# Attention and multiplicative feed-forward in float32: two-level gates from the fifth group on, and ScalarE's copies around the DMA turns

## The chip, the cores and the metric

The kernel runs on one core of a Trainium2 chip. The metric is the device time of one execution in microseconds (us), taken as the median over runs; lower is better. One execution was also recorded instruction by instruction, and all views below are of that one.

## The reference

Eight batches of linear attention with 8 heads of 64, 576 tokens each, an RMS norm per head, and then a feed-forward block on the 4608 tokens. All is float32.

```python
kv  = np.einsum('bhsd,bhse->bhde', k, v)
out = np.einsum('bhsd,bhde->bhse', q, kv)
rms = np.sqrt(np.mean(out * out, axis=-1, keepdims=True) + 1e-06)
x   = (out / rms * g_norm)             # then (B,H,S,D) -> (B*S, H*D) = 4608 x 512
a = x @ w1                             # 512 x 1024
b = x @ w2                             # 512 x 1024
h = a * b @ w3                         # 1024 x 1024
return h @ w_out                       # 1024 x 512
```

## The kernel before, in words

The product of w3 and w_out is folded into one matrix `w3o` at the start, so that each token needs the **gates** (x@w1 times x@w2, elementwise) and the **projection** (gates @ w3o). The tokens are worked on in nine groups of 512: groups 0 to 6 are the first 512 tokens of batches 0 to 6, then comes group 8 (the 64 tokens left over of every batch), and last group 7. Only the first group's order differs.

A group is one chain of TensorE (PE) work. The gates have 1024 columns, cut into four blocks p = 0..3 of 2 x 128. A block is done by `gates`, which calls `winograd`: a Strassen-Winograd scheme of one level, 7 products in place of 8, each of 4 matmuls 128x256. The sums that the scheme needs are made by VectorE: of the weights once (`sum_w`, kept in `ws0` to `ws3`), of x per group (`combine_x`, kept in `xc`), of the gates per block (`sum_ab`). ScalarE (ACT) takes three or four of the products out of PSUM (`keep`), and VectorE adds and multiplies the others (`done`, `multiply`). After the four blocks, `project_twice` makes the projection in two levels, 7 times 7 products of 2 matmuls 128x128; `sum_inner` makes its inner sums on VectorE, and the inner sums of w3o are loaded from HBM by `load_b` into three buffers (`streams`), 896 KB each.

In the last two groups (`TWICE`, 8 and 7) blocks 0 and 1 are made together in two levels by `gates_of_two`: two halves w (w1 and w2), each of 7 outer products of 7 matmuls 128x128. There the inner sums of the weights come from HBM (`prepare_w` writes them to `w_l2` in groups 3 and 4, `load_w` brings them back in three parts of 896 KB into the same three buffers), and the inner sums of x are made on GpSimd (POOL) by `sum_x` in 28 small operations. Order there: block 2, then blocks 0 and 1 in two levels, then block 3, then the projection.

While group T runs, the attention of batch T+1 is worked in between. `steps` makes eight lists of work, one for each call of `between`: `begin_kv` (k^T v), `finish` (q times kv and the norm, by `product` and `norm`), in odd batches `product_left` for the tokens left over of two batches. The norm is an ACT square into a tile `sq`, a VectorE reduction, an ACT square root, a VectorE reciprocal and a VectorE multiply that frees the PSUM bank. x and q are turned (transposed) by DMA: `turn_by_dma` copies a tile apart in 16-bit words, SyncE (SP) issues the DMA that turns it, and a second copy puts it together. All those copies but a few in the first group are POOL's.

[...] five of the pool `mm`, three of the pool `at`. A bank is handed out in turn, so a use waits for the readers of the use five (or three) back. PE, POOL and SP run in the order in which the code issues; VectorE and ACT are ordered by a scheduler, except where the code sets an order by hand.

Of the kernel before, what the change touches and what calls it, by code (L numbers as in the profile page):

```python
# [22 lines left out]
def kernel(  # L23
# [40 lines left out]
    KF = DF // P  # L64
    NH = KF // 2
# [254 lines left out]
    def attention(b):  # L320
# [41 lines left out]
        def q_by_dma(r):  # L362

            qT[r] = work.tile([P, 2, 2, P], FP32, name="qT")
            q_sb = loaded["q", b, r].rearrange("p e n -> p (e n)")
            to = qT[r].rearrange("p e i t -> p (e i t)")
            return turn_by_dma([q_sb], to, q_sb, [to], q_copy)
# [3 lines left out]
        def q_left_by_dma():  # L371
            st["qT"] = work.tile([P, NP, P], FP32, name="qT_left", bufs=1)
            src = q_left[b // 2].rearrange("p h d -> p (h d)")
            to = st["qT"].rearrange("p r t -> p (r t)")
            return turn_by_dma([src], to, src, [to], q_copy)

        def norm(o_ps, dsts):

            n, w = len(o_ps), o_ps[0].shape[1]
            inv = work.tile([P, n, w // D], FP32, name="inv")  # L380
            for i in range(n):
                sq = work.tile([P, G], FP32, name="sq")[:, 0:w]
                nc.scalar.activation(sq, o_ps[i], AF.Square)  # L383
                nc.vector.tensor_reduce(  # L384
                    out=inv[:, i], in_=sq.rearrange("p (h d) -> p h d", d=D), axis=AX.X, op=ALU.add
                )
            yield
            nc.scalar.activation(inv, inv, AF.Sqrt, scale=1.0 / D, bias=eps_col)
            yield
            nc.vector.reciprocal(inv, inv)  # L390
            for i in range(n):
                m, k = dsts[i].shape[1:3]
                nc.vector.tensor_tensor(  # L393
                    out=dsts[i],
                    in0=o_ps[i].rearrange("p (m k d) -> p m k d", k=k, d=D),
                    in1=inv[:, i].rearrange("p (m k) -> p m k", k=k).unsqueeze(3).to_broadcast(
                        [P, m, k, D]
                    ),
                    op=ALU.mult,
                )  # L400
# [24 lines left out]
        def product_left():  # L425
# [3 lines left out]
            o_ps = [bank(ps_at, "at"), bank(ps_mm, "mm")]  # L429
# [23 lines left out]
        def x_by_dma(h, copy=nc.gpsimd.tensor_copy):  # L453

            xn, x = st[h].rearrange("p i l m d -> p (i l) (m d)"), xT[b][:, h]
            flat = x.rearrange("p i r n -> p (i r n)")
            turned = st[h].rearrange("p i l m d -> p (i l m d)")
            half = [slice(r * G, (r + 1) * G) for r in range(2)]
            return together(
                turn_by_dma(  # L460
                    [xn[:, :, r * P:(r + 1) * P]], flat[:, half[r]], turned[:, half[r]], [x[:, :, r]],
                    copy,
                )
                for r in range(2)
            )

# [37 lines left out]
        def finish(h):  # L504
# [4 lines left out]
            q_two_by_dma, q_left_by_dma, x_by_dma, x_left_by_dma,  # L509
# [4 lines left out]
    def batch(b):  # L514
        if b not in batches:
            batches[b] = attention(b)
        return batches[b]

    def steps(b):
# [25 lines left out]
        odd = b % 2  # L545
        if b == 1:
# [12 lines left out]
        if b == 1:  # L559
# [19 lines left out]
            ends[5].append((end, "left", "u3"))  # L579
        else:  # L580
# [8 lines left out]
        if odd:  # L589
            fs[second].append((a.product_left,))  # L590
        if b == 1:
            turn(6, a.x_by_dma, 1)
            turn(7, a.x_left_by_dma, next_group=True)
        else:
            turn(5, a.x_by_dma, 1)
            if odd:
                turn(5, a.x_left_by_dma, next_group=more)
        if more:
            turn(7 if b == 1 else 5, batch(b + 1).q_two_by_dma, 0, 1, next_group=True)
            fs[7 if odd else 0].append((load_q_left, b + 1))  # L600
# [38 lines left out]
    def winograd(lhsT, rhs, chunks, done, between=lambda: None, keep_u3=True):  # L639
# [17 lines left out]
        def keep(name, ps):  # L657
            t = late_tile(name)[:, 0:4, :].rearrange("p (u a) n -> p u (a n)", u=2)
            copies.setdefault(name, []).append(nc.scalar.copy(t, ps))  # L659
            late[name] = t  # L660
# [109 lines left out]
    def gates(T, p, between, ready=lambda name: None):  # L770
# [4 lines left out]
        def multiply(name, one, two):  # L775

            dst = ab[int(name[1]) - 1][:, p, int(name[2]) - 1, :]
            if two is None:
                c = late_pool.tile([P, N], FP32, name="c21")
                nc.scalar.copy(c, one[:, 0, :])  # L780
# [15 lines left out]

    def prepare_w():

        for n, (name, _) in enumerate(PRODUCTS):
# [5 lines left out]
            for i, s in enumerate((s1, s2, s4)):  # L805
                at = (3 * n + i) * 2 * P
                nc.sync.dma_start(
                    out=w_l2[:, at:at + 2 * P].rearrange("p (w m) -> p w m", w=2), in_=s
                )
            yield  # L810

    def replace_a21():
        for name, _ in PRODUCTS:
            a11, _, a21, _ = w_blocks(name)
            nc.vector.tensor_sub(a21, a11, a21)

    loaded_w = []

    def load_w():
        n = len(loaded_w)  # L820
        t = streams[(n + 1) % len(streams)]
        nc.sync.dma_start(out=t, in_=w_l2[:, n * PART:(n + 1) * PART])
        loaded_w.append(t)
# [3 lines left out]
    def sum_x(T):  # L827
        if not x_sums:
            for name in ("k_sb", "v_sb", "q_sb"):
                for _ in range(2):  # L830
                    x_sums.append(inp.tile([P, 2, J * D], FP32, name=name))
            x_sums.append(work.tile([P, 2, 2, P], FP32, name="qT"))
            x_sums[:] = [
                t.rearrange("p a b -> p (a b)") if len(t.shape) == 3 else
                t.rearrange("p a b c -> p (a b c)") for t in x_sums
            ]
            x_sums[:] = [[t[:, i * P:(i + 1) * P] for i in range(4)] for t in x_sums]
        nc.gpsimd.tensor_copy(tick, late["p1"][:, 0, 0:1])
        for t, (_, name) in zip(x_sums, PRODUCTS):
            b11, b12, b21, b22 = (  # L840
                xb[T][name][:, c, i * P:(i + 1) * P] for c in range(2) for i in range(2)
            )
            t1, t2, t3, t4 = t
            nc.gpsimd.tensor_sub(t1, b12, b11)
            nc.gpsimd.tensor_sub(t2, b22, t1)
            nc.gpsimd.tensor_sub(t3, b22, b12)
            nc.gpsimd.tensor_sub(t4, b21, t2)

    places = []

    def gates_of_two(T):

        if not places:
            other = work.tile([P, 2, 2, NP // 2, N], FP32, name="xT")
            other = other.rearrange("p i j r n -> p (i j r n)")
            places.extend([other[:, 0:PART // 2], other[:, 1024:1024 + PART // 2]])
            places[:] = [t.rearrange("p (n t) -> p n t", t=P) for t in places]

        def products(n, w, ps, new):
            a_name, b_name = PRODUCTS[n]  # L860
            a11, a12, s3, a22 = (t[:, w] for t in w_blocks(a_name))
            s1, s2, s4 = (
                loaded_w[q // 7][:, q % 7 * 2 * P + w * P:q % 7 * 2 * P + (w + 1) * P]
                for q in range(3 * n, 3 * n + 3)
            )
# [3 lines left out]
            t1, t2, t3, t4 = x_sums[n]  # L869
# [10 lines left out]
            if w == 1 and n in (2, 4, 6):  # L880
                load_b()
            return ps

        def banks(pool, tag):
            return [bank(pool, tag).rearrange("p (i n) -> p i n", n=P) for _ in range(2)]

        def keep(t, ps):
            nc.scalar.copy(t[:, 0:4], ps[0])
            nc.scalar.copy(t[:, 4:7], ps[1][:, 0:3])
# [22 lines left out]
        for w in range(2):  # L912
            r1 = products(0, w, banks(ps_mm, "mm"), True)
            p1 = keep(late_tile("p1"), r1)
            r3 = products(1, w, banks(ps_at, "at"), True)
# [3 lines left out]
            z = keep(late_tile("u2"), r1)  # L919
            r2 = products(3, w, banks(ps_mm, "mm"), True)  # L920
            p5 = keep(places[1] if w else late_tile("p5"), r2)
# [7 lines left out]
            finish(keep(places[0], r1), w, 1, 0)  # L929
# [110 lines left out]
    def project_twice(T, last, ahead, load_after):  # L1040
# [43 lines left out]
        def keep(name, ps):  # L1084
            t = late_tile(name)
            nc.scalar.copy(t[:, 0:4], ps[0])  # L1086
            nc.scalar.copy(t[:, 4:7], ps[1][:, 0:3])
            return t

        def finish(z, half, j):  # L1090
# [8 lines left out]
            nc.vector.tensor_add(dst[:, 0], z[:, 3:6:2], z[:, 0:3:2])  # L1099
# [89 lines left out]
    w_l2 = dram.tile([P, 3 * PART], FP32, name="w_l2")  # L1189
    PRODUCTS = [  # L1190
        ("a11", "b11"), ("a12", "b21"), ("s2", "t2"), ("s1", "t1"), ("s3", "t3"), ("s4", "b22"),
        ("a22", "t4"),
    ]
    TWICE = (B, B - 1)

# [103 lines left out]
    for n, T in enumerate(groups):  # L1299
        pieces = steps(T + 1) if n + 2 < NG else iter([])  # L1300

        def between():
# [8 lines left out]
            if T == B - 2 and p == 2 and not replaced:  # L1311
                replaced.append(True)
                replace_a21()

        if T in TWICE:
            once = iter([T])
            gates(T, 2, lambda: [sum_x(t) for t in islice(once, 1)])
            run(sum_ab(2))
            in_order = tc.manual_schedule(engines={mybir.EngineType.DVE})
            in_order.__enter__()  # L1320
            gates_of_two(T)
# [3 lines left out]
        for p in range(NF):  # L1325
            if T in TWICE and p + 1 < NF:
                continue
            if T and p + 1 == NF:
# [10 lines left out]
                if T in TWICE:  # L1339
                    following["c12"] += of_two[:1]  # L1340
                    following["c22"] += of_two[1:]
                else:
# [38 lines left out]
            else:  # L1381
                ops = [step() for step in sum_ab(p)]
                with tc.issue_after(ops[-1].ins):
                    for _ in range({(3, 1): 2, (3, 2): 2, (4, 1): 2, (4, 2): 1}.get((T, p), 0)):
                        next(preparing_w)
        last = n + 1 == NG
        if T:
            project_twice(
                T, last, [] if last else combine_x(groups[n + 1]),
                load_w if not last and groups[n + 1] in TWICE else load_b,  # L1390
# [38 lines left out]
```

## Time and profile before

| what | value |
|---|---|
| median of 3 runs | 758.41 us (758.13 to 759.74) |
| the profiled execution | 758.72 us, its span 756.9 us |
| PE busy | 749.4 us of the span (99%) |
| VectorE busy | 589.4 us (78%) |
| ACT busy | 267.0 us (35%) |
| POOL busy | 164.1 us (22%) |
| HBM | 165 GB/s over the span |

Between the span and the execution's time lie 1.8 us that no instruction covers. "Busy" counts the time in which an engine executes; the mean granted clock of PE is 1.000. In lines of groups, `x` is the count of instructions; a float32 matmul of the program is recorded as two, so that one of 128x256 stands for 2 records.

### The profile page before, as it was taken

The numbers are of one execution on the slowest core, as the hardware profiler recorded it, in microseconds if no ns is written. First come the engines' busy times: TensorE is split into PE (matmuls) and PEld (weight loads), VectorE is DVE, ScalarE is ACT, GpSimd is POOL, SyncE is SP. The second block draws the span as 40 slices with busy tenths as digits, with TensorE's granted clock in tenths as the row PEclk, the third lists the DMA queues.
The fourth block names the chain that finished last, engine by engine and source line by source line (L and its number), as shares of the span: only waits on it lengthen the run. The fifth ranks groups of instructions, "written<-read, shape, count | busy, mean of one in ns | idle before, by whom it ended". The sixth has DMA issues, their size and how long they took to land.

```text
span 756.9 us, 14948 instructions
## 1 busy us (share of the span) xinstructions
PE 749.4 (99%) x5903; PEld 657.7 (87%) x5903; DVE 589.4 (78%) x1171; ACT 267.0 (35%) x492; POOL 164.1 (22%) x190
## 2 busy tenths in 40 slices
PE   8999999999999999999999999999999999999998
PEld 5455788888899889988998899889988999999997
DVE  7977999639888568758975897567776778996897
ACT  6777787312322232223222322232223223222321
POOL 0000000322511441144114410431143124006000
PEclk9999999999999999999999999999999999999999
DMA  9996954349997845675767567745743470465244
GB/s 319 344 334 177 273 163 102 85 104 271 336 299 248 225 114 177 223 205 141 218 218 210 155 192 223 208 103 173 224 125 53 150 225 28 146 211 186 87 152 139
DMA packets 146554, 143.20 MB, mean 189 GB/s; under 512 B 86580, under 2 KB 133812, under 8 KB 146484
## 3 DMA queue, kind: packets, MB, share of 16 engines
q1 hardware_dynamic: 144032, 127.82, 58.1%
q10 hardware_dynamic: 2452, 14.42, 5.7%
q8 instruction: 47, 0.77, 0.4%
q14 instruction: 23, 0.19, 0.1%
HBM read 105.78 MB, written 19.14 MB: 165 GB/s over the span
## 4 chain that ended last, share of the span: by engine, by line
PE 97%; DVE 1%; DMA 1%; ACT 1%; issue 0%; SPq 0%; ACTq 0%
PE mm L646 55%; PE mm L1075 23%; PE mm L625 7%; PE mm L875 5%; PE at L339 3%; PE at L415 2%; PE at L612 1%; PE at L875 1%; DMA raw<-in_moe_w_out_dram 1%; PE at L1126 0%; DVE ab L163 0%; PE at L358 0%; PE at L434 0%; DVE chunks L170 0%; SPq L198 0%
## 5 line engine op out<-in xcount | busy, mean ns | idle before, releaser
L646 PE MATMUL mm<-xT,w_sb 128*128 128x256 f32 x720 | 165.2, 380 | 0.0
L646 PEld LDWEIGHTS mm<-xT,w_sb 128*128 128x128 f32 x720 | 136.6, 191 | 18.3 <-issue 0.5
L646 PE MATMUL mm<-xc,ws 128*128 128x256 f32 x512 | 116.2, 380 | 0.0
L646 PEld LDWEIGHTS mm<-xc,ws 128*128 128x128 f32 x512 | 97.3, 190 | 13.7 <-ACT p L659 0.8
L296 POOL COPY xT<-xn 128x1024 uint16<-128x1024 uint16 x26 | 31.2, 1227 | 171.9 <-DVE xn L393 171.9
L784 DVE TENSOR_TENSOR c<-mm,u 128x512 f32<-128x512 f32 x32 | 22.0, 689 | 58.4 <-PE mm L646 58.4
L659 ACT COPY u<-mm 128x512 f32<-128x512 f32 x58 | 34.0, 585 | 93.4 <-PE mm L646 82.8
L659 ACT COPY p<-mm 128x512 f32<-128x512 f32 x66 | 38.7, 586 | 73.9 <-PE mm L646 68.5
L646 PE MATMUL mm<-xc,w_sb 128*128 128x256 f32 x256 | 61.4, 383 | 0.0
L625 PE MATMUL mm<-chunks,ab 128*128 128x512 f32 x128 | 60.1, 603 | 1.0 <-DVE chunks L173 1.0
L646 PE MATMUL mm<-xT,ws 128*128 128x256 f32 x240 | 57.4, 383 | 0.0
L785 DVE TENSOR_TENSOR ab<-c 128x256 f32<-128x256 f32 x96 | 53.8, 561 | 2.5
L646 PEld LDWEIGHTS mm<-xc,w_sb 128*128 128x128 f32 x256 | 48.0, 190 | 6.9 <-ACT u L659 0.3
L646 PEld LDWEIGHTS mm<-xT,ws 128*128 128x128 f32 x240 | 45.1, 190 | 6.2
L1075 PE MATMUL mm<-w3o_sb,ab 128*128 128x128 f32 x368 | 48.7, 276 | 0.0
L1075 PE MATMUL mm<-w3o_sb,raw 128*128 128x128 f32 x372 | 48.1, 276 | 0.0
L384 DVE TENSOR_REDUCE inv<-sq 128x8 f32<-128x512 f32 (+1 forms) x40 | 23.4, 627 | 30.0 <-ACT sq L383 30.0
L1075 PEld LDWEIGHTS mm<-w3o_sb,ab 128*128 128x128 f32 x368 | 45.4, 192 | 0.5
L780 ACT COPY c<-mm 128x256 f32<-128x256 f32 x32 | 11.9, 372 | 95.4 <-PE mm L646 95.4
L1075 PEld LDWEIGHTS mm<-w3o_sb,raw 128*128 128x128 f32 x372 | 44.8, 192 | 0.0
L1086 ACT COPY u<-mm 128x512 f32<-128x512 f32 x23 | 13.5, 586 | 85.3 <-DVE raw L1099 46.6
L310 POOL COPY xT<-xn 128x1024 uint16<-128x1024 uint16 x26 | 31.6, 1244 | 54.0 <-DMA xn<-xT 54.0
(300 smaller groups left out, 1378.7 us busy)
## 6 DMA issues: line engine op xcount, KB each, us to landing
w3o_sb<-w3o_l SPq DMA_DIRECT2D x18, 896.0 KB, 5.4
raw<-in_moe_w_dram SPq DMA_DIRECT2D x31, 512.0 KB, 7.1
raw<-w3o_l SPq DMA_DIRECT2D x15, 896.0 KB, 4.7
w3o_sb<-w3o_l ACTq DMA_DIRECT2D x14, 896.0 KB, 4.6
k_sb<-in_k_dram SPq DMA_DIRECT2D x32, 256.0 KB, 4.5
v_sb<-in_v_dram SPq DMA_DIRECT2D x32, 256.0 KB, 4.7
q_sb<-in_q_dram SPq DMA_DIRECT2D x32, 256.0 KB, 3.3
out_dram<-raw SPq DMA_DIRECT2D x14, 512.0 KB, 4.3
```

What stands on the lines that cost most here:

```text
L296: copy(to, src.rearrange("p a n w -> p w a n"))
L310: copy(words(dst), src)
L339: nc.tensor.matmul(kv_ps[e * D:(e + 1) * D, r - rs[0], :], lhsT=k_sb[:, e, cols] if j < J else kl[:, 2 * r + e, :], rhs=v_sb[:, e, cols] i ...
L384: nc.vector.tensor_reduce(out=inv[:, i], in_=sq.rearrange("p (h d) -> p h d", d=D), axis=AX.X, op=ALU.add)
L415: nc.tensor.matmul(o_ps[l][tokens, n * D:(n + 1) * D], lhsT=qT[r][rows, e, i, tokens], rhs=kv_b[rows, e, r, :], start=True, stop=True,)
L625: nc.tensor.matmul(sums_ps[half][m], lhsT=w3T[half, c][:, m, :], rhs=chunks[:, c, 1, :], start=(c == 0), stop=(c == KF - 1),)
L646: nc.tensor.matmul(ps[:, u, :], lhsT=lhsT(a_name, u, c), rhs=rhs(b_name, c),  start=(u == 0 and c == 0 and to is None), stop=(c == chunks ...
L659: copies.setdefault(name, []).append(nc.scalar.copy(t, ps))
L784: adds.setdefault(name, []).append(nc.vector.tensor_add(c, one, two))
L785: nc.vector.tensor_mul(dst, c[:, 0, :], c[:, 1, :])
L875: nc.tensor.matmul(ps[place // 4][:, place % 4, :], lhsT=x, rhs=y, start=new and place // 4 not in seen, stop=True, skip_group_check=True,)
L1075: nc.tensor.matmul(to[:, i, :], lhsT=x[:, c, :], rhs=y[:, c, :], start=new and place // 4 not in seen, stop=(c == 1), skip_group_check=True,)
```

## The change

Six parts belong together.

1. `IN_TWO` replaces `TWICE` for the two-level gates: groups 4, 5, 6, 8 and 7 make blocks 0 and 1 by `gates_of_two`. In groups 4, 5 and 6 the attention of batches 5, 6 and 7 is worked in at the same eight places, now two in block 2, four in `gates_of_two` and two in block 3. `product_left` moves from the fifth place to the sixth, and in those batches takes both its banks from the pool `at`.
2. `sum_x` is made by VectorE in 8 large operations and runs ahead of block 2. Its results lie in `ws0` and `ws1`, and in a new tile `xs`.
3. As `ws0` and `ws1` are taken, the outer sums of the weights of blocks 0 and 1 are streamed too: 66 blocks of 64 KB in `w_l2`, loaded in five parts (four of 896 KB, one of 640 KB) per group. Parts 3 and 4 are loaded within `gates_of_two`, as soon as the buffers of parts 0 and 1 are done with. `load_b` for the projection is called three times at the end of `gates_of_two`.
4. `prepare_w` and `replace_a21` write `w_l2` in groups 2 and 3, in 33 stores in place of 21.
5. In batches 5, 6 and 7 the copies around the DMA turns of x and q are ACT's. They are put behind named ACT copies out of PSUM (`slots`, `run_slot`, `turns_by_scalar`). Only the turn of the tokens left over stays with POOL.
6. `gates_of_two` takes its five banks from `mm` alone, by a written plan; the tile `sq` has one buffer in place of two, in all groups.

```diff
+    FIRST_OF_TWO = 4
...
-        def q_by_dma(r):
+        def q_by_dma(r, copy=None):
...
-            return turn_by_dma([q_sb], to, q_sb, [to], q_copy)
+            return turn_by_dma([q_sb], to, q_sb, [to], copy or q_copy)
...
-                sq = work.tile([P, G], FP32, name="sq")[:, 0:w]
+                sq = work.tile([P, G], FP32, name="sq", bufs=1)[:, 0:w]
...
-            o_ps = [bank(ps_at, "at"), bank(ps_mm, "mm")]
+            o_ps = [bank(ps_at, "at"), bank(*((ps_at, "at") if b > FIRST_OF_TWO else (ps_mm, "mm")))]
...
+    def run_slot(key, behind):
+        for f, *args in slots.pop(key, []):
+            with tc.issue_after(behind.ins):
+                f(*args)
+
+    def turns_by_scalar(b):
...
+        for r in (2, 3):
+            at((0, 0), begin, ("q", b, r), a.q_by_dma, r)
+        if b % 2:
+            at(("p2", "c21"), begin, ("q", "left"), a.q_left_by_dma)
+            at((0, 3), end, ("q", "left"))
+        at((0, 6), end, ("q", b, 2))
+        at((1, 0), end, ("q", b, 3))
+        for h, begins, ends in (
+            (0, ((0, 3), (0, 3)), ((1, 3), (1, 3))),
+            (1, (("p3", "p1"), ("p3", "p5")), (("p3", "c21"), ("proj", "p1"))),
+        ):
+            for r in range(2):
+                at(begins[r], begin, ("x", h, r), a.x_part_by_dma, h, r)
+                at(ends[r], end, ("x", h, r))
+        if b + 1 < B:
+            n = batch(b + 1)
+            for r in range(2):
+                at(("p3", "u2"), begin, ("q", b + 1, r), n.q_by_dma, r)
+                at(("proj", ("u2", "u3")[r]), end, ("q", b + 1, r))
...
+        elif by_scalar:
+            turns_by_scalar(b)
...
-            fs[second].append((a.product_left,))
+            fs[5 if by_scalar else second].append((a.product_left,))
...
-        nc.gpsimd.tensor_copy(tick, late["p1"][:, 0, 0:1])
-        for t, (_, name) in zip(x_sums, PRODUCTS):
...
-            nc.gpsimd.tensor_sub(t1, b12, b11)
...
+        whole = xT[T].rearrange("p i j c n -> p (i j) c n"), xc
+        for (t1, t2, t4, t3), x in zip(x_sums, whole):
+            b11, b12, b21, b22 = (x[:, :, c, i * P:(i + 1) * P] for c in range(2) for i in range(2))
+            nc.vector.tensor_sub(t1, b12, b11)
+            nc.vector.tensor_sub(t2, b22, t1)
+            nc.vector.tensor_sub(t3, b22, b12)
+            nc.vector.tensor_sub(t4, b21, t2)
...
+        mm = [bank(ps_mm, "mm").rearrange("p (i n) -> p i n", n=P) for _ in range(5)]
+        plan = [((0, 1), (2, 3), (4, 2)), ((3, 4), (2, 0), (1, 2))]
+        names = [("p1", "u2", "p5", "p1"), ("p5", "p1", "u2", "p5")]
...
-            if w == 1 and n in (2, 4, 6):
-                load_b()
+            load(w, n)
+            if n in (2, 5):
+                between()
...
+        def load(w, n):
+            last = max(at for (v, m, _), at in BLOCKS.items() if (v, m) <= (w, n))
+            if last + 1 >= (len(loaded_w) - len(streams) + 1) * IN_PART:
+                load_w()
+            if (w, n) == (1, len(PRODUCTS) - 1):
+                for _ in range(3):
+                    load_b()
...
+    IN_TWO = (*range(FIRST_OF_TWO, B - 1), *TWICE)
...
-            if T == B - 2 and p == 2 and not replaced:
+            if T == FIRST_OF_TWO - 1 and p == 2 and not replaced:
...
-        if T in TWICE:
-            once = iter([T])
-            gates(T, 2, lambda: [sum_x(t) for t in islice(once, 1)])
+        if T in IN_TWO:
+            p = 2
+            stage[0] = "p2"
+            with tc.issue_after(adds["out"].ins):
+                sum_x(T)
+            gates(T, p, between)
...
-            gates_of_two(T)
+            gates_of_two(T, between)
...
-                    for _ in range({(3, 1): 2, (3, 2): 2, (4, 1): 2, (4, 2): 1}.get((T, p), 0)):
+                    for _ in range({(2, 0): 1, (2, 1): 2, (2, 2): 2, (3, 0): 1, (3, 1): 1}.get((T, p), 0)):
```

## The prediction

> **What bounds the kernel now.** I read the page's busy times, then the chain of work that ended last, then the sums by window, one row per group. Groups 4, 5 and 6 are the first three rows; the fourth is group 8, which already has the two-level gates.
>
> ```profile
> PE 749.4 (99%) x5903; PEld 657.7 (87%) x5903; DVE 589.4 (78%) x1171; ACT 267.0 (35%) x492; POOL 164.1 (22%) x190
> PE 97%; DVE 1%; DMA 1%; ACT 1%; issue 0%; SPq 0%; ACTq 0%
> ```
>
> ```profile
> core 0: us, PE busy (x) PEld busy (x) DVE busy (x) ACT busy (x) POOL busy (x), PEclk, DMA share, GB/s
> 391.40:466.92 75.52, 75.39 (x658) 68.85 (x657) 58.80 (x120) 20.73 (x45) 22.79 (x20) 1.00 0.68 193
> 466.92:542.36 75.44, 75.44 (x630) 68.93 (x629) 50.97 (x108) 20.27 (x43) 19.75 (x19) 1.00 0.61 175
> 542.36:617.09 74.73, 74.73 (x622) 68.07 (x621) 54.46 (x120) 20.18 (x42) 20.90 (x20) 1.00 0.48 136
> 617.09:685.04 67.95, 67.95 (x506) 65.11 (x505) 57.32 (x128) 18.57 (x35) 13.69 (x29) 1.00 0.46 152
> ```
>
> The reader is to see that PE has no idle time in these groups, and that VectorE (DVE) is the next engine. A group's time is its PE work; it can fall only if PE gets less work, and only while DVE and ACT keep up.
>
> The PE timeline gives both prices: block 3 of group 8, on one level, runs from the first line to the last.
>
> ```profile
> 629.18 0.61 PE L875 MATMUL mm<-x_left,w_sb 128*128 128x128 f32 x4
> ...
> 651.07 1.89 PE L646 MATMUL mm<-x_left,w_sb 128*128 128x256 f32 x8
> ...
> 663.15 1.05 PE L1075 MATMUL mm<-w3o_sb,ab 128*128 128x128 f32 x8
> ```
>
> One block costs 663.15 - 651.07 = 12.08 us, two cost 24.16. In two levels the same two cost 651.07 - 629.18 = 21.89: 14 outer products of 1.56 us.
>
> [...] the same operation beside POOL's work and then without it.
>
> ```profile
> 627.34 0.56 DVE L785 TENSOR_TENSOR ab<-c 128x256 f32<-128x256 f32 x1
> ...
> 629.13 0.42 DVE L785 TENSOR_TENSOR ab<-c 128x256 f32<-128x256 f32 x1
> ```
>
> [...] The trace has 686 to 689 (c at L784, beside nothing) and 548 to 555 (L1115), and I use the trace's. [...] the page's busiest slice has 344.
>
> **Part by part.**
>
> *PE.* Three groups change level: 3 x (24.16 - 21.89) = 6.8 us less. Moved attention work keeps its PE time.
>
> *VectorE, groups 4 to 6.* Durations alone: 128x128 0.29, 128x256 0.42, 128x384 0.55, 128x512 0.69. Removed with two blocks: 6 sums c (4.1), 6 products (2.5), 2 of c21 (0.8), 8 of `sum_ab` (3.4): 10.8. Added: 8 x sums (4 x 0.69 + 4 x 0.55 = 5.0), 6 pairs of `add` (7.4), 8 `finish` of 0.29 + 3 x 0.42 (12.4), 4 products (2.8), 4 of `sum_ab_two` (2.8): 30.4. Net 19.6. Group 5's own durations sum to 54.9, of which 3.1 are slowdown beside POOL (each operation against its median without POOL). So 54.9 - 3.1 + 19.6 = 71.4; in groups 4 and 6, with the left-over norm of odd batches (2 x 0.42 + 0.19 + 2 x 0.41 = 1.9), 73.3. Durations overlap: from 617.09 to 688 they sum to 64.7 but cover 60.05, so 73.3 covers 68.0. To this comes a gap of 0.03 us before each operation that needs its predecessor, some 75 times: 2.3. VectorE needs 70.3 us of a group of 75.5 - 2.3 = 73.2, or 96%. It fits on the whole; what counts is where it is late.
>
> *Sums of x ahead of block 2.* Hidden: between the last projection work and block 2's first sum VectorE waited 4.31 us at the start of group 7, and the eight need 4.4 at the observed dispatch. Without that cover it would push c12 back by at most 4.4.
>
> *Where PE will wait.* I followed the order of instructions with these durations and with 0.23 to 0.25 us from a product's end to its reader (block 3's first product ends at 651.07 + 1.72; ACT copies it at 653.00).
>
> (a) `product_left`, groups 4 and 6. Its second bank is now the first bank of `product(1)`, freed by the first norm multiply. From the start of half 1: product(1) ends at 18.0 - 10.9 = 7.1. The chain is square (0.6), reduction (0.68), second square, which with one `sq` waits for that reduction and stands behind half a `keep`, second reduction, then on ACT the other half keep (0.48) and an x copy (1.16), square root (0.31), then VectorE's reciprocal, a `finish` step, an `add` (0.6) and the multiply: done at 13.2. PE gets there at 11.8. Wait: **1.4 us each, 2.8 for two**. Queued behind it on PE are the last product of half 1 and block 3. Bounds: 0 if ACT's x copy is not ahead of the square root and VectorE is free earlier, 3 each if an ACT copy waits for its DMA turn.
>
> (b) Block 2's last bank: the second outer product needs the bank that c21's multiply reads. Two reductions stand ahead of it, the second 0.6 later for the single `sq`. It is free 1.7 us after block 2, PE wants it at 1.56: **0.15 us in three groups, 0.5**. Bounds 0 and 1.
>
> (c) End of the gates. VectorE reaches block 3's c12 with no lag in groups 4 and 6 (PE was held in (a)), about 0.3 late in group 5; the projection's first sums had 0.35 us to spare in group 8. **0.2**; bounds 0 and 2 per group.
>
> *ACT.* 20.3 us per group plus 16 to 18 copies of 1.05 or 1.16 (its rows at L296 to L310): 18 to 20; eight keeps of 1.07 for six of 0.59 and two of 0.37: 4. About 43 of 73: hidden, but one copy in front of a keep costs up to 1.16 of the 1.56 to 3.1 us until PE reuses the bank. By the order they fit, with about 0.5 to spare. POOL keeps the left-over turn; one copy of 1.38 in block 3 may delay VectorE by up to 0.85. I take 0 beyond (a) to (c), bounds 0 and 3 in all.
>
> *Weights streamed.* Groups 4 to 6 get 4.2 MB each: at 344 GB/s 12 us more of DMA in 73; the 0.61 share becomes about 0.8. SP's order puts part 3 behind two q turns (1.3 us of issue each) and ahead of x's. It leaves at about 6.6 us of `gates_of_two`, and its first block is wanted at 14.7: 8.1 us. The page has:
>
> ```profile
> w3o_sb<-w3o_l SPq DMA_DIRECT2D x18, 896.0 KB, 5.4
> ```
>
> Hidden; under the crowded DMA of group 1 such a load took 8.3 us, so up to 0.2 to 2 us per group, five times, if that returns. I take 0. Parts 0 to 2 replace projection loads at the same places, and part 4 has over 3 us to spare.
>
> *Writing `w_l2`.* Fifteen more VectorE operations in group 2 (0.42 to 1.3 each: 6 to 13 us) where 55.1 of 75.9 us are busy; group 3 trades 12 sums for 7 replaced ones plus 6. The stores are 12 more, 0.36 us of SP each. Hidden; 0 to 1.
>
> *Groups 8 and 7.* PE work as before; sums of x move from POOL to VectorE into the idle 4.3 us. 0; bounds -0.2 and 0.5.
>
> **Sum.** -6.8 + 2.8 + 0.5 + 0.2 = **-3.3 us**. The profiled execution would go from 758.7 to 755.4; it lies 0.3 above the median, so 755.1.
>
> **Rivals.**
>
> *R1, no new waits.* VectorE's chain is quicker than (a) says. For it: group 8 ran the same gates with PE 67.95 of 67.95 busy. Against it: no norm stood in that VectorE queue. Gives 758.4 - 6.8 = 751.6.
>
> *R2, VectorE becomes the bound.* It is 96% loaded in order, with norms and their ACT round trips between two-level sums whose bank PE wants within 1.56 us. If each group loses more than 2.3 us of PE time, the change loses. With every one of about 148 operations at full duration and no overlap (73.3 and 71.4) plus the norm's waits (about 1.5 per norm, 3 per group) groups take about 76.3, 74.4 and 76.3: 227.0 against 225.7. With 2 us more per group for ACT and bank lags: 233, or +7. I give 758.5 to 765, centre 760. For it: c12's wait on PE in block 3 was only 0.28 us in group 8. Against it: the overlap is seen everywhere in group 8.
>
> *R3, weights arrive late*, over 8.1 us after issue. Five groups of 1 us: 5 us lost, so 756.8 to 760 together with (a). For it: DMA share 0.8. Against it: 4.4 to 6.3 us in groups 5 to 8.
>
> **Numbers.** A difference of about 0.2%, or 1.5 us, is what a measurement can tell from none. Forecast (752.8 to 757) 0.50; R1 0.16; R2 0.20; R3 0.14. Faster: 0.50 x 0.98 + 0.16 + a third of R3 = 0.70; same: half of R3 and a fifth of R2, 0.11; slower: the rest, 0.19. The range 751.6 to 760 leaves out R2's upper half and R1's edge; the forecast alone is 752.8 to 757.
>
> **What would show it.** In the profile after: 588 matmul records of 128x128 in the two-level gates of groups 4 to 6, and groups 4, 5 and 6 at about 74.8, 73.5 and 74.0 us (before less 2.27, plus the waits); PE's waits on VectorE at `product_left`, twice, 1 to 2 us; VectorE busy near 68 in each; POOL almost empty from group 4; no PE wait on a DMA. Wrong: PE idle over 7 us in groups 4 to 6, or a wait on `w_l2`.

## The result, and the profile after

The changed kernel takes 765.85 us (median of 4 runs, 765.04 to 766.03) where the kernel before takes 758.53 beside it: a ratio of 1.0092, 95% interval 1.0074 to 1.0109. It is slower by 7 us; the prediction said 755.1, and 760.0 at most.

The profiled execution is 765.04 us with a span of 763.3, 6.4 more than before. The page after, busy times and then the chain of work that ended last:

```profile
PE 747.2 (98%) x6155; PEld 658.8 (86%) x6155; DVE 642.3 (84%) x1301; ACT 322.1 (42%) x558; POOL 83.1 (11%) x83
...
PE 79%; DVE 12%; ACT 5%; issue 2%; DMA 1%; POOL 0%; SPq 0%; ACTq 0%; DVEq 0%; POOLq 0%
```

PE's busy time fell by 2.2 us (749.4 before) and not by 6.8. Short waits between matmuls are in part counted as busy: with the same 6155 records, a kernel below that waits less (a_both) shows 744.2. What counts more is that the chain, 97% PE before, now passes for 12% through VectorE and for 5% through ACT: PE waits. The sums by window, one row for each of groups 2, 4, 5, 6 and 8:

```profile
core 0: us, PE busy (x) PEld busy (x) DVE busy (x) ACT busy (x) POOL busy (x), PEclk, DMA share, GB/s
241.10:320.74 79.64, 76.67 (x662) 69.24 (x661) 66.09 (x129) 21.14 (x46) 22.35 (x20) 1.00 0.72 207
396.74:472.99 76.25, 74.83 (x746) 70.27 (x745) 68.19 (x151) 41.40 (x70) 4.41 (x4) 1.00 0.80 230
472.99:546.96 73.97, 73.45 (x714) 69.42 (x713) 65.06 (x146) 38.85 (x65) 2.44 (x3) 1.00 0.80 238
546.96:622.48 75.52, 73.83 (x706) 69.15 (x705) 67.27 (x150) 36.36 (x62) 2.67 (x3) 1.00 0.62 200
622.48:690.94 68.46, 68.26 (x507) 64.90 (x506) 60.45 (x137) 18.51 (x35) 0.00 (x0) 1.00 0.51 173
```

In groups 4 to 6 PE is idle for 1.42, 0.52 and 1.69 us; the largest idle time, 79.64 - 76.67 = 2.97, is in group 2, which still runs on one level. The list of PE's waits (engine and line, releaser; us in total, times, longest) names who is late:

```profile
PE mm L699 <- ACT p L712: 4.6, 10, 1.0
...
PE mm L699 <- DVE c L839: 1.8, 1, 1.8
PE at L435 <- DVE xn L394: 1.3, 2, 0.6
```

L712 is `keep`, L839 the sums on VectorE, L435 `product_left`. No wait for a DMA is in the list. The whole list of the kernel before has nothing of the kind, only three waits in the first 20 us:

```profile
PE mm L277 <- POOL ident masks.py:199: 2.0, 1, 2.0
PE mm L625 <- DVE chunks L173: 1.0, 1, 1.0
PE at L612 <- DVE chunks L173: 0.8, 1, 0.8
```

The table cuts the span of the profiled execution at the first product of each group, for every kernel that ran; the span's end is taken to 0.1 us, as the pages give it. Its first line is the kernel before; the others show the difference to it, in us. The last column is the median over the runs against that of the kernel before beside it, as a ratio with its 95% interval.

| kernel | start, groups 0, 1 | group 2 | group 3 | groups 4 to 6 | groups 8, 7 | ratio |
|---|---|---|---|---|---|---|
| before | 238.72 | 76.50 | 75.44 | 226.43 | 139.81 | |
| changed | +2.4 | +3.1 | +0.6 | -0.7 | +1.0 | 1.0092 (1.0074 to 1.0109) |
| b_sq1 | +2.6 | -0.1 | 0 | +1.2 | 0 | 1.0048 (1.0033 to 1.0063) |
| b_prep | +2.1 | +0.2 | 0 | +0.1 | +0.1 | 1.0010 (1.0003 to 1.0017) |
| b_sq1_prep | +3.0 | +3.1 | +0.6 | -0.1 | 0 | 1.0094 (1.0079 to 1.0110) |
| a_first7 | +2.3 | +3.3 | +0.6 | -0.1 | +1.1 | 1.0094 (1.0080 to 1.0108) |
| a_sq2 | -0.4 | -0.1 | 0 | -0.7 | +0.9 | 1.0008 (0.9999 to 1.0016) |
| a_alias | +2.9 | +2.1 | +0.6 | -4.3 | 0 | 1.0027 (1.0020 to 1.0035) |
| a_both | -0.3 | +0.5 | 0 | -4.2 | 0 | 0.9948 (0.9936 to 0.9961) |
| a_left | +0.4 | +0.5 | 0 | -4.1 | -0.1 | 0.9953 (0.9941 to 0.9966) |
| a_order | +1.3 | +0.3 | 0 | -3.9 | 0 | 0.9955 (0.9941 to 0.9968) |
| a_prep | +0.1 | -0.2 | +0.6 | -4.2 | -0.1 | 0.9944 (0.9932 to 0.9957) |

The first column holds chance: the first 20 us wait for the conversion of the weights that are being loaded (0.4 to 1.9 us in these traces), so a difference of 1 us there in a single trace means little. In b_prep PE also waits 1.0 us for loads of w3o's sums at the end of group 1, ahead of anything that its edit moves, and its profiled execution (761.14 us) is the slowest of its 20: its +2.1 is chance too. The other columns repeat within 0.3 us between kernels that share the edit, but for group 2, where up to 1 us is chance too (see a_alias).

So the loss has three places: the groups ahead of the two-level ones (6.1 us), the last two groups (1.0), and groups 4 to 6, which gained 0.7 in place of 3.3. Theory A: each is a buffer that is read late, and they are the single `sq`, the writing of `w_l2` in group 2, and the tiles p1 and p5 of block 3. Theory B: VectorE is too full in groups 4 to 6, and the start differs by chance.

### The profile page after: what moved, and what is told of

Its sections match the earlier page's. It is cut to its first block, busy times and chain, and to the rows that moved or that the text cites. A ratio compares the mean times of both kernels' runs of the same rounds, so it can differ in the third digit from the quotient of the medians.

```text
span 763.3 us, 15602 instructions
## 1 busy us (share of the span) xinstructions
PE 747.2 (98%) x6155; PEld 658.8 (86%) x6155; DVE 642.3 (84%) x1301; ACT 322.1 (42%) x558; POOL 83.1 (11%) x83
## 4 chain that ended last, share of the span: by engine, by line
PE 79%; DVE 12%; ACT 5%; issue 2%; DMA 1%; POOL 0%; SPq 0%; ACTq 0%; DVEq 0%; POOLq 0%
PE mm L699 36%; PE mm L1162 22%; PE mm L953 11%; PE mm L678 5%; PE at L340 2%; PE at L416 2%; DVE inv L385 1%; DVE c L839 1%; ACT xT L311 1%; DVE ab L995 1%; DVE ab L164 1%; ACT sq L384 1%; DVE p L991 1%; DVE xn L394 1%; DVE c L992 1%
## 5 line engine op out<-in xcount | busy, mean ns | idle before, releaser
L699 PE MATMUL mm<-xT,w_sb 128*128 128x256 f32 x576 | 132.2, 379 | 0.0
L699 PEld LDWEIGHTS mm<-xT,w_sb 128*128 128x128 f32 x576 | 108.7, 190 | 14.8 <-issue 0.5
L699 PE MATMUL mm<-xc,ws 128*128 128x256 f32 x416 | 96.0, 381 | 3.0 <-ACT p L712 3.0
L699 PEld LDWEIGHTS mm<-xc,ws 128*128 128x128 f32 x416 | 78.3, 190 | 16.5 <-ACT p L712 6.2
L712 ACT COPY u<-mm 128x512 f32<-128x512 f32 x46 | 27.0, 587 | 69.4 <-PE mm L699 59.7
L712 ACT COPY p<-mm 128x512 f32<-128x512 f32 x54 | 31.3, 585 | 56.8 <-PE mm L699 38.2
L699 PE MATMUL mm<-xc,w_sb 128*128 128x256 f32 x208 | 50.1, 384 | 1.8 <-DVE c L839 1.8
L699 PE MATMUL mm<-xT,ws 128*128 128x256 f32 x192 | 46.1, 383 | 1.4 <-ACT p L712 1.4
L699 PEld LDWEIGHTS mm<-xT,ws 128*128 128x128 f32 x192 | 35.8, 190 | 7.6 <-ACT p L712 2.8
L678 PEld LDWEIGHTS mm<-chunks,ab 128*128 128x128 f32 x128 | 21.8, 190 | 23.9 <-issue 15.3
L840 DVE TENSOR_TENSOR ab<-c 128x256 f32<-128x256 f32 x78 | 40.2, 515 | 2.1
L953 PE MATMUL mm<-ws,w3o_sb 128*128 128x128 f32 x250 | 38.5, 275 | 0.0
L839 DVE TENSOR_TENSOR c<-mm,u 128x512 f32<-128x512 f32 x26 | 17.8, 685 | 21.0 <-PE mm L699 20.9
```

What stands on the lines that cost most here:

```text
L678: nc.tensor.matmul(sums_ps[half][m], lhsT=w3T[half, c][:, m, :], rhs=chunks[:, c, 1, :], start=(c == 0), stop=(c == KF - 1),)
L699: nc.tensor.matmul(ps[:, u, :], lhsT=lhsT(a_name, u, c), rhs=rhs(b_name, c),  start=(u == 0 and c == 0 and to is None), stop=(c == chunks ...
L839: adds.setdefault(name, []).append(nc.vector.tensor_add(c, one, two))
L840: nc.vector.tensor_mul(dst, c[:, 0, :], c[:, 1, :])
L953: nc.tensor.matmul(ps[place // 4][:, place % 4, :], lhsT=x, rhs=y, start=new and place // 4 not in seen, stop=True, skip_group_check=True,)
```

## The experiments

### One buffer for sq, alone: b_sq1

```diff
-                sq = work.tile([P, G], FP32, name="sq")[:, 0:w]
+                sq = work.tile([P, G], FP32, name="sq", bufs=1)[:, 0:w]
```

In the kernel before.

> The kernel before, with one buffer in place of two for the tile sq. Theory A (the changed kernel loses by buffers that are read late): the second square of every norm waits for the first reduction and holds ACT meanwhile, so PE loses what it lost in the changed kernel before group 2 (2.4 us), and a little in later groups: 760.9 to 762.5 us. Theory B (the loss is VectorE's load in groups 4 to 6, and the 2.4 us at the start are chance): within 1 us of 758.5.

Measured: 762.38 us, 3.6 more: inside A's range, and far outside B's. The ACT timeline of b_sq1 in group 0 (start, duration, engine and line; in brackets the idle time before and its releaser):

```profile
113.65 0.60 ACT L383 ACTIVATE sq<-at 128x512 f32<-128x512 f32 x1
115.06 0.60 ACT L383 ACTIVATE sq<-at 128x512 f32<-128x512 f32 x1 [0.81 <-DVE inv L384]
115.55 0.37 ACT L780 COPY c<-mm 128x256 f32<-128x256 f32 x1
116.41 0.31 ACT L388 ACTIVATE inv<-inv,eps_col 128x16 f32<-128x16 f32 x1 [0.49 <-DVE inv L384]
116.62 1.05 ACT L659 COPY p<-mm 128x512 f32<-128x512 f32 x2
```

and what PE does meanwhile:

```profile
117.24 1.99 PE L646 MATMUL mm<-xc,ws 128*128 128x256 f32 x8 [0.79 <-ACT p L659]
```

The second square writes `sq` only when VectorE's reduction has read it, and ACT waits 0.81 us for that. In these traces ACT takes its instructions in the order that was set, so everything behind it waits as well: the square root (116.41), and two `keep` copies (116.62) that free banks for the gates. The wait belongs to the norm, the price is paid by the gates. In the trace three such places ahead of group 2 delay PE's products by 0.30, 0.75 and 0.80, together 1.9 us. Another 1.2 lies in group 4: there PE waits for a sum (`[1.06 <-DVE c L784]`) ahead of which three operations of `prepare_w` stand in VectorE's order, at its old place. Neither theory had foreseen that, and it leads to b_sq1_prep.

### w_l2 written earlier, alone: b_prep

```diff
-                    for _ in range({(3, 1): 2, (3, 2): 2, (4, 1): 2, (4, 2): 1}.get((T, p), 0)):
+                    for _ in range({(2, 0): 1, (2, 1): 2, (2, 2): 2, (3, 0): 1, (3, 1): 1}.get((T, p), 0)):
```

In the kernel before.

> The kernel before, with the seven steps of prepare_w moved to groups 2 and 3 as in the changed kernel; nothing else. Theory A: in group 2 six VectorE operations stand beside POOL's copies ahead of block 3's first sum, and PE waits there some 2 us, so 760 to 761.5 us. Theory B: VectorE has room in group 2, 758 to 759.

Measured: 759.53, that is 0.7 more than the kernel before beside it: between the two ranges. Group 2 loses only 0.2. So of the 3.1 us that group 2 lost in the changed kernel, neither edit by itself brings any: b_sq1 has -0.1 there, b_prep +0.2.

### Both: b_sq1_prep

> The kernel before with both: one buffer for sq, and the blocks of w_l2 made in groups 2 and 3. Alone the first cost 3.6 us and the second 0.7. Theory A (each tightens the same chain in group 2: three operations of prepare_w at 1.14 to 1.25 us stand in VectorE's order ahead of the two reductions, and with one sq the second square, and ACT's keep behind it, waits for them): more than the sum, +6.5 to +8 us, with PE stalls of over 1 us in block 1 and block 3 of group 2 as in the changed kernel; about 765 to 766.5. Rival B (the two losses add up, and group 2 of the changed kernel was slow for something else in the change): +4.3, about 763.

Measured: 765.6, +7.1, where the sum of the two is +4.3. Theory A holds: where the two meet they cost more than their sum. This kernel, with no two-level gates in groups 4 to 6 and no other part of the change, has the time of the changed kernel (there the -0.7 and +1.0 of the later groups nearly cancel), and group 2 and group 3 are longer by the same 3.1 and 0.6. Group 4 is back at -0.1, because `prepare_w` no longer stands there. How it comes about is seen in the changed kernel. The plainer of two places is block 1 of group 2, ACT's timeline and then PE's:

```profile
258.23 0.60 ACT L384 ACTIVATE sq<-at 128x512 f32<-128x512 f32 x1 [3.54 <-DVE inv L385]
```

```profile
260.42 1.99 PE L699 MATMUL mm<-xc,ws 128*128 128x256 f32 x8 [1.01 <-ACT p L712]
```

Three operations of `prepare_w` (1.25, 1.14 and 1.14 us, beside a POOL copy) stand ahead of the first reduction in VectorE's order. So the second square waits 3.54 us, the `keep` behind it is late, and PE loses 1.1 us. In b_sq1, without the three operations, the square waits 0.81 and PE not at all; in b_prep, with them but with two buffers, the square need not wait for the reduction, and PE loses 0.2. The other 2.1 us of group 2 are lost in block 3. VectorE's timeline there (L753 makes sums of gates, `sum_ab`):

```profile
289.61 1.25 DVE L753 TENSOR_TENSOR ab<-ab 128x256 f32<-128x256 f32 x1
290.79 1.37 DVE L753 TENSOR_TENSOR raw<-ab,raw 128x256 f32<-128x256 f32 x1
292.08 1.37 DVE L875 TENSOR_TENSOR raw<-ws 128x256 f32<-128x256 f32 x1
...
294.71 0.41 DVE L877 TENSOR_TENSOR raw<-w_sb,w3o_sb 128x256 f32<-128x256 f32 x1
295.04 0.68 DVE L839 TENSOR_TENSOR c<-mm,u 128x512 f32<-128x512 f32 x1
...
296.28 0.69 DVE L839 TENSOR_TENSOR c<-p,mm 128x512 f32<-128x512 f32 x1
```

PE's, and POOL's a little earlier:

```profile
297.03 1.99 PE L699 MATMUL mm<-xc,w_sb 128*128 128x256 f32 x8 [1.83 <-DVE c L839]
```

```profile
287.14 1.10 POOL L299 COPY qT_left<-xn_left 128x1024 uint16<-128x1024 uint16 x1 [2.80 <-DVE xn_left L394]
```

Six sums of `prepare_w` (L875 to L877) stand ahead of the two sums at L839; the second, which ends at 296.97, frees the bank that PE waits for. Besides, VectorE works beside POOL's copies: of the four sums of gates and the six of `prepare_w`, five take 0.93 to 1.37 us in place of 0.42. Two lines of b_prep, the first of the same six and the sum behind them:

```profile
289.14 0.41 DVE L802 TENSOR_TENSOR raw<-ws 128x256 f32<-128x256 f32 x1
...
291.15 0.68 DVE L784 TENSOR_TENSOR c<-mm,u 128x512 f32<-128x512 f32 x1
```

There that sum starts 50.4 us after the group's start, here 53.9, and PE does not wait in this block: the slack just holds. With one `sq` the norms reach VectorE later: the norm of the left-over tokens ends 45.9 us after the group's start, in b_prep 41.1. POOL's copies wait for it (2.80 us in the line above), so they fall on VectorE's sums, five slowed ones in place of two (1.04 and 1.37 us). By these durations POOL's slowing makes about 2.4 of the 3.5 us, an estimate that no run tested by itself. The scheduler put the six there in both.

### The second square put elsewhere: a_sq2

```diff
+    second_sq = const.tile([P, G], FP32, name="xs")
...
-                sq = work.tile([P, G], FP32, name="sq", bufs=1)[:, 0:w]
+                sq = (second_sq if i and b <= FIRST_OF_TWO else work.tile([P, G], FP32, name="sq", bufs=1))[:, 0:w]
...
-                late_pool.tile([P, 4, P], FP32, name="xs"),
+                second_sq.rearrange("p (n t) -> p n t", t=P),
```

In the changed kernel. The second `sq` had given its 2 KB to the new tile `xs`; as no sum of x is made before group 4, the norms of batches 0 to 4 can have that place.

> The changed kernel; norms of batches 0 to 4 put their second square into the tile xs, which is idle until group 4. Theory A: the 2.4 us before group 2 and the 1.2 us wait in group 2's second block go, 761.8 to 762.8 us. Theory B: 765.3 to 766.3.

Measured: 759.38, 6.5 less than the changed kernel, outside both ranges and about twice what A expected, since the expectation did not know how the two losses add. Up to group 3 the kernel now has the times of before, within 0.4 us. `prepare_w` still stands in group 2 and costs nothing there.

### Block 3's tiles in another turn: a_alias

```diff
-            t = late_tile(name)[:, 0:4, :].rearrange("p (u a) n -> p u (a n)", u=2)
+            place = dict(p1="u2", p5="p1", u2="p5")[name] if stage[0] == "p3" else name
+            t = late_tile(place)[:, 0:4, :].rearrange("p (u a) n -> p u (a n)", u=2)
```

In the changed kernel. The reason is in its ACT timeline, start of block 3 in group 4:

```profile
440.87 0.59 ACT L712 COPY p<-mm 128x512 f32<-128x512 f32 x1 [1.94 <-DVE c L993]
...
443.46 0.59 ACT L712 COPY p<-mm 128x512 f32<-128x512 f32 x1 [1.06 <-DVE c L993]
```

and PE's:

```profile
441.50 1.99 PE L699 MATMUL mm<-xc,ws 128*128 128x256 f32 x8 [0.19 <-ACT p L712]
444.10 1.99 PE L699 MATMUL mm<-xT,ws 128*128 128x256 f32 x8 [0.60 <-ACT p L712]
```

ACT does not wait for PE's product, it waits for VectorE's line 993, the end of `finish`: half 1 holds its last sums in the tiles p1 and p5, and block 3 wants to keep its first two products in tiles of the same names. The edit gives block 3's first product the tile u2, which `finish` is done with first.

> The changed kernel; in block 3 of the groups with two-level gates the three kept products go to the tiles u, p1, p5 in the order in which VectorE is done with them, in place of p1, p5, u. Theory A: ACT no longer waits for VectorE's last two finishes at the start of block 3; PE's waits there (about 1.1, 0.7, 1.2, 0.5, 0.5 us in groups 4, 5, 6, 8, 7) mostly go: 762 to 763.5 us. Theory B: VectorE is late anyway, PE waits at c12, c22 or the projection in its place, 765 to 766.

Measured: 761.16, 4.7 less than the changed kernel, again more than A expected. Groups 4 to 6 are now 4.3 us shorter than before in place of 0.7, groups 8 and 7 have lost nothing. Some 1.1 us of the profile's gain is group 2, where the edit changes no order: there a POOL copy that waits for its DMA started 0.9 us later in the group, and only one of three `prepare_w` operations ran beside it (1.14 us, the others 0.42 and 0.43). I take that part for chance. It tells something all the same: with the single `sq`, and the three operations where they were, the second square waits 1.99 us in place of 3.54, and PE's wait in block 1 is gone. So in these traces that loss came about only where POOL slowed VectorE as well.

### The two-level gates undone: a_first7

```diff
-    FIRST_OF_TWO = 4
+    FIRST_OF_TWO = 7
```

> The changed kernel with FIRST_OF_TWO = 7: groups 4, 5 and 6 make all blocks on one level and their copies on POOL again, product_left at its old place, the rest of the change stays. Theory A (the start and groups 0 to 3 lose about 6.1 us to sq and w_l2, groups 8 and 7 about 1.0 to the tiles p1 and p5; the two-level groups together were 0.7 faster than before): about 766 to 767, the time of the changed kernel or up to 1 us more. Rival B (the two-level gates of groups 4 to 6 are what costs, VectorE being full): 760 to 762, as the loss goes with them.

Measured: 765.75, just under A's range. Without the two-level gates of groups 4 to 6 and ACT's copies there, the time is that of the changed kernel. B's 760 to 762 is out: what makes the kernel slower is not in those groups.

### Both repairs: a_both

> The changed kernel with the second square of the norms of the first five batches in the tile xs, and block 3's tiles p1, u2 and p5 taken in another turn. Theory A (the two losses have nothing to do with each other, 6.5 and 4.7 us): 654 records of gain left, that is 765.85 - 11.2 = 754.7, range 754 to 756: the kernel is then faster than before by about 4 us, near the 6.8 us of PE work saved less 1.7 for the bank at product_left and about 1 of small waits. Rival B (VectorE is nearly full in groups 4 to 6, and repairing one wait only uncovers the next): 757.5 to 759.

("654 records of gain left" is a slip of the pen there; the sum beside it is meant.) Measured: 754.82 us (754.57 to 755.49), ratio 0.9948 (0.9936 to 0.9961): faster than both kernels, and within 0.2 us of A's sum. The windows of groups 4, 5 and 6 in a_both:

```profile
390.81:465.80 74.99, 74.36 (x746) 70.50 (x745) 68.01 (x150) 41.44 (x70) 4.42 (x4) 1.00 0.81 233
465.80:538.96 73.16, 73.16 (x715) 69.59 (x714) 65.16 (x147) 38.90 (x65) 2.56 (x3) 1.00 0.79 240
538.96:613.02 74.06, 73.32 (x706) 69.33 (x705) 66.83 (x150) 36.43 (x62) 2.42 (x3) 1.00 0.63 203
```

VectorE is as busy as in the changed kernel (68.01, 65.16 and 66.83 us for 68.19, 65.06 and 67.27), and yet PE's idle time falls from 1.42, 0.52 and 1.69 us to 0.63, 0 and 0.74. So VectorE's load was not the limit; what it was late with was.

### product_left: a_left and a_order

What is left in a_both is mainly PE's wait at `product_left` in groups 4 and 6. The profile shows 0.63 us of idle time; from one start to the next it is 0.82 us more than usual. Two edits of a_both try to remove it. a_left issues it one outer product later:

```diff
-            if n in (2, 5):
+            if (w, n) in ((0, 2), (0, 5), (1, 2), (1, 6)):
```

> As a_both, and product_left is issued one outer product later (after the last of half 1 and not before it). Theory A (PE waits 0.85 us twice there for the bank that the first norm multiply frees; 1.56 us later it is free): 1.0 to 1.7 us less than a_both, about 753 to 754.5. Rival B (the wait passes on, because the norm of the left-over tokens then stands in VectorE's and ACT's order beside block 3's first sums): the same as a_both within 0.4 us.

Measured: 755.39, no gain (0.6 more than a_both; B allowed 0.4). The wait at `product_left` is gone, but in block 3 PE waits. PE's timeline of a_left, where between the lines nothing waits:

```profile
430.75 0.69 PE L436 MATMUL at<-kv_sb,qT_left 64*64 64x64 f32 x32
...
439.23 3.07 PE L700 MATMUL mm<-xT,w_sb 128*128 128x256 f32 x13 [0.68 <-ACT p L714]
```

and those of ACT and VectorE:

```profile
438.59 0.59 ACT L714 COPY p<-mm 128x512 f32<-128x512 f32 x1 [1.55 <-PE mm L700]
```

```profile
437.24 1.26 DVE L995 TENSOR_TENSOR c<-p 128x256 f32<-128x256 f32 x1
```

The profile names a product as what ACT waited for, but the product that it copies, block 3's third, had its last matmul start at 436.4 and was long done. What ends at 437.24 + 1.26 = 438.50 is the last `finish`, which reads the tile that this keep writes. It is late because the norm of the left-over tokens now stands ahead of it in VectorE's order (0.20 and 0.75 us from 435.84 on), and because it runs beside POOL's left-over copy. Rival B's mechanism is the right one here, and the bound is once more a tile. a_order keeps the place, and issues the products into the free bank ahead of those into the other (8 products each, 16 records):

```diff
-            for r in range(NP):
-                for l in range(2):
-                    for e in range(2):
+            order = [(r, l, e) for r in range(NP) for l in range(2) for e in range(2)]
+            if b > FIRST_OF_TWO:
+                order.sort(key=lambda k: k[2])
+            for r, l, e in order:
```

> As a_both, but product_left in batches 5 and 7 issues its 16 products into the free bank first and then the 16 into the bank that the first norm multiply frees; before they alternate. Theory A (PE waits 0.82 us there because the second of the 32 already needs that bank): 16 products of about 0.02 to 0.03 us fill 0.35 to 0.5 of each wait, so 0.7 to 1.0 us less than a_both, about 753.9. Rival B (as when the whole step was issued later: ACT and VectorE are then the late ones, and block 3 waits for them instead; or the products of one half no longer run side by side with those of the other): within 0.3 us of a_both.

Measured: 755.77, no gain: the kernel before took 759.22 beside it, and 758.47 beside a_both, so they are 3.45 and 3.65 us faster than it. PE's timeline in a_both and then in a_order:

```profile
428.52 0.32 PE L436 MATMUL at<-kv_sb,qT_left 64*64 64x64 f32 x2
429.47 0.69 PE L436 MATMUL at<-kv_sb,qT_left 64*64 64x64 f32 x30 [0.63 <-DVE xn L395]
```

```profile
429.95 0.68 PE L437 MATMUL at<-kv_sb,qT_left 64*64 64x64 f32 x16
430.91 0.68 PE L437 MATMUL at<-kv_sb,qT_left 64*64 64x64 f32 x16 [0.28 <-DVE xn L395]
```

The wait fell from 0.63 to 0.28, but 16 records of one half take as long as 30 that alternate between the halves: those ran side by side. B's second reason holds. From the first record of `product_left` to the next gate product it is 1.57 us in both kernels.

### prepare_w moved within a_both: a_prep

The steps at (2,1): 2, (2,2): 1, (3,0): 2, (3,1): 2.

> As a_both, with the 7 steps of prepare_w at (2,1): 2, (2,2): 1, (3,0): 2, (3,1): 2, so that none stands after block 0 of group 2, where three of its operations delayed block 1's keep. Theory A (group 2 has 0.46 us left of that): group 2 at 76.5 in place of 76.96, 0.4 us less in all. Rival B (group 3 takes the two steps and has norms of its own): the same or up to 0.5 us more, with the loss in group 3.

Measured: 754.82, the figure of a_both, though the kernel before was 0.7 slower beside it; the intervals of the ratios overlap, so the medians do not decide. The profiles do: against a_both group 2 wins 0.7 us, and group 3 loses 0.6. B holds: the sums cost some 0.6 us next to a norm, in whichever of the two groups that is.

## Why the prediction was wrong, point by point

- **Where the sum went.** The forecast was -3.3 us, all of it in groups 4 to 6; the span rose by 6.4. Of these 9.7 us, 6.1 lie ahead of group 4, 2.6 in groups 4 to 6 and 1.0 in groups 8 and 7.
- **PE, -6.8 us**: right. Group 5 of a_both has no idle PE and is 75.44 - 73.16 = 2.28 us shorter; the step said 2.27. The 588 records are there. Of the 2.6 us that groups 4 to 6 of a_both lack to 6.8, the wait at `product_left` is 1.6 and a late VectorE sum in group 6's projection 0.4. "Moved attention work keeps its PE time" is not quite so: PE's starts are farther apart where it goes over to `product_left` and back, now that the step no longer follows `product(1)` directly: in group 4 of a_both 0.32 us in place of 0.22 on the way there (428.20 to 428.52) and 0.55 in place of 0.44 after it (430.09 to 430.64). For two groups that is 0.4 us, most of the rest.
- **"Writing `w_l2` ... Hidden; 0 to 1"**: the first failed step. Alone it is right (0.7). But it was costed against VectorE's average in group 2 (55.1 of 75.9 us busy), and against the kernel before; the same change takes a buffer from the norm whose operations stand in the same queue. Together they cost 3.5 us more than `sq` alone (765.6 against 762.38 for b_sq1).
- **One `sq` buffer**: the second failed step, by omission. The prediction saw the mechanism (in (a): the second square "waits for that reduction") and priced it in groups 4 to 6 only, although the front says "in all groups". In groups 0 to 3 nothing was put down, and no reason was given. It costs 3.6 us alone.
- **(a) `product_left`, 1.4 each**: the right mechanism, sized too high: 0.82 each. Issued later or in another order the step cost the same.
- **(b) block 2's last bank, 0.5**: no PE interval at the second outer product is longer than usual by over 0.1 us in any of the three groups. Too high.
- **(c) end of the gates, 0.2**: the third failed step. It followed block 3's banks and not the SBUF tiles into which its keeps go. PE's intervals around block 3 and into the projection's first products are longer by 1.1 us in group 4, 0.7 in group 5 and 1.5 in group 6: 3.3 in place of 0.2.
- **Groups 8 and 7, 0, at most 0.5**: the same tiles; 1.0 for the two.
- **ACT 0, weights streamed 0**: right, ACT is busy for 36 to 41 us of 74 to 76 and waits for others; DMA share 0.80, 0.80 and 0.62, parts of `w_l` land in 5.2 us, no PE wait on a DMA. R3 is out.
- **R1** hoped for too much: once the tiles are repaired, groups 4 to 6 gain 4.2 us, between its 6.8 and the forecast's 3.3. **R2** had the sign, and a range to 765 that almost holds the time, but not the mechanism: VectorE's load of 65 to 68 us is the same in a_both, which wins.
- **Two lines misread.** The row of group 4 starts at 391.40, but PE's first product of that group starts at 390.66: the group before takes 76.26 us and not 75.52. And in the pair that is to show VectorE with and without POOL, POOL works in both. Beside the second, of 0.42 us, stand two POOL operations:

```profile
628.77 0.46 POOL L846 TENSOR_TENSOR q_sb<-x_left 128x128 f32<-128x128 f32 x1
629.19 0.69 POOL L847 TENSOR_TENSOR q_sb<-x_left,q_sb 128x128 f32<-128x128 f32 x1
```

There it is POOL's operation that is slow, 0.69 us where 38 of its 56 subtractions take 0.45 or 0.46. So in these traces the slowing falls on VectorE (0.56 us in place of 0.42) or on POOL (0.69 in place of 0.46), and the example gave too small a size for it.

The groups' own forecast (74.8, which is 75.5 from the group's true start, 73.5 and 74.0) was met or bettered by a_both with 74.99, 73.16 and 74.06, though partly because errors cancel: (a) and (b) were too high by 1.6 us together, and about 1.0 came from what had been put at next to nothing. What failed was where it looked: all signs that it named lie in groups 4 to 6, and 6.1 of the 6.4 us that the span lost lie ahead of them. That PE waits inside group 2 behind `prepare_w` in the form above is shown by b_prep, b_sq1 and b_sq1_prep; POOL's share in it rests on the durations of the traces and on a_alias, and no run was made to part it from that of the six operations themselves.

## What to carry to other kernels

A buffer that is dropped in every stage to make room in one must be priced in every stage (the single `sq` alone cost 3.6 us), and its price is not the wait itself but what is queued behind the waiting instruction on its engine (in block 1 of group 2 a square that waited 3.54 us cost PE 1.1). A wait that makes an operation late can also move it beside another engine's work that slows it (in block 3 of group 2, five slowed sums in place of two). Follow tiles in SBUF with the same care as PSUM banks: here a name that was used again was a wait for the last reader of its last use (1.94 and 1.06 us of ACT in block 3 of group 4). Two edits that are each hidden can share one reserve (in group 2 -0.1 and +0.2 us alone, +3.1 together); cost them together, in the queue where they meet.

## What the runs showed of the hardware

The 32 matmul records 64x64 of `product_left` take 0.69 us when they alternate between the two halves of the rows (a_left), and 16 of one half take 0.68 by themselves (a_order). A VectorE sum of two operands with 128x256 elements, 0.42 us alone, took 0.93 to 1.38 us beside POOL's copies of 16-bit words (changed kernel, group 2), far more than the 0.56 beside POOL's small subtractions in the prediction's example.
